# Two rows of v on SyncE's ring, a small transpose moved behind the K/Q transposes, the fp32 identity copied by VectorE, and four numbers of the scheduler's model altered

## Chip, cores and metric

One core of one Trainium2 chip. The metric is the device time of one execution in microseconds (us). Times are medians of several executions; a ratio is the mean time of one kernel's fast runs over the mean of the other's fast runs in the same rounds on the same chip, so it isn't quite the ratio of the medians quoted, and it carries a 95% interval. A difference counts as faster or slower from 2% on. A trace is of one single execution.

## The reference

Causal attention with a decay for 8 batches of 8 heads, 576 tokens and head size 64, then RMS norm and a gated feed-forward layer over the 4608 tokens.

```python
def _attn_ref(q, k, v, s):                       # q, k, v: (8, 8, 576, 64), s: (8, 8, 576)
    scores = scale * np.matmul(q, k.transpose(0, 1, 3, 2))
    cum = np.cumsum(np.maximum(s, 0.0), axis=-1)
    bias = -(cum[:, :, :, None] - cum[:, :, None, :])
    scores = np.where(causal, -1000000000.0, scores + np.minimum(bias, 0.0))
    ...                                          # softmax over keys
    return np.matmul(attn, v)

def _moe_ref(x, w_gate, w_val, w_out, rms_g):    # x: (4608, 512), d_ff 1536
    xn = x / np.sqrt(np.mean(x * x, axis=-1, keepdims=True) + 1e-06) * rms_g
    g = xn @ w_gate
    return (g * (1.0 / (1.0 + np.exp(-g))) * (xn @ w_val)) @ w_out
```

## The kernel before

The kernel isn't written in the order in which it runs. Every operation is recorded with the engine, a key (its priority) and modelled durations; a list scheduler plays the engines, the DMA and the PSUM banks through with these durations, and emits each engine's instructions in the order that it found. Where the model leaves TensorE idle in the first 24 us, `spin` puts fillers on a tile of zeros.

```python
class Plan:
    def schedule(self):                  # cut
        ...
            if o.dma:
                begin = max(self.dma_free, s + o.us + o.lags[0])
                self.dma_free = begin + o.dma
                o.done = self.dma_free + o.lags[1]

def load_runs(b, which, h0, h1, key, part=0):          # K (which 0) or Q (1) of four heads
    us = ((1.2, 1.25)[part] * (h1 - h0) / 4) if b == 0 else 3.05 * (h1 - h0) / 8
    return I("pool", "dma_start", 0.7, key=key, dma=us, lags=(1.1, 1.2), ...)

def prep_transpose(b, hp, key, part=0):                # K and Q of two heads, through PSUM
    mms(..., [...  ident_bf ...], key=key)             # then one copy by VectorE, one by ScalarE

# the beginning
kqa = [load_runs(0, w, h, h + 4, -100) for h in range(0, H, 4) for w in range(2)]
ident(ident_bf, -99.5)                                 # GpSimd
kqb = [load_runs(0, w, h, h + 4, -92, part=1) for h in (0, 4) for w in range(2)]
v0 = load_rows(v_nat[0], v, 0, "pool", -94)
ident(ident_F, -93.7)                                  # GpSimd
...                                                    # weight loads, fills by VectorE
wP = decay(-95)
for hp in range(HP):
    prep_transpose(0, hp, -80 + hp)
for hp in range(HP):
    prep_transpose(0, hp, -65 + hp, part=1)
gp_ = bank("g", 1)
mms(0.1, [(gp_[:, 0:CC], g4, ident_F[0:CC, 0:CC], True, True, True)], key=-75)
...
# per chunk c of 512 tokens: feed-forward, and beside it attention of batch c + 1
            if b < NRUN:                               # batch 1: K and Q transposed by TensorE
                for hp in range(HP):
                    prep_transpose(b, hp, K + hp)
            else:
                prep_cast(b, K - 14)                   # later batches: by DMA, on SyncE
...
                I("sp", "dma_start", 0.62, key=key, dma=0.75, out=out[rows, cols], in_=o[:, 0:w])

    def spin(b):
        nc.tensor.matmul(b[:, 0:256], lhsT=still[:, 0:128], rhs=still, start=True, stop=True)
```

## Time and profile before

| | before |
|---|---|
| time, median of 3 runs | 358.78 us (358.7 to 360.33) |
| span of the profiled run | 356.3 us |
| TensorE busy | 96% of the span |
| first K/Q transpose of batch 0 | 8.00 us |
| first feed-forward matmul | 23.50 us |
| K/Q transposes of batch 1 done | 44.49 us |
| feed-forward number 200, just behind the beginning of the second chunk | 68.82 us |
| last matmul ends | 351.95 us |

The feed-forward matmuls with the gate and value weights are counted in the trace (1248 of them) from 0 in order of start; the second chunk begins with number 192.

### The profile page before, as it was taken

What the parts mean: (1) busy time and instruction counts of PE and PEld (TensorE: products, weight loads), DVE (VectorE), ACT (ScalarE), POOL (GpSimd) and SP (SyncE); (2) the same over time, 40 slices, a digit from 0 to 9 for tenths busy, and PEclk for the clock granted to TensorE, in tenths of its full rate; (3) what the DMA queues carried; (4) which work ended last, traced back from release to release, by engine and by line L of the source; (5) the groups of instructions that cost most, each with busy time, mean ns of one, the idle gap of its engine ahead of it and who ended that gap; (6) DMA issues with size and microseconds to landing.
All of it is one profiled execution on the core that took longest, in us unless ns stands there. A gap on an engine that the chain in (4) does not pass through costs nothing.

```text
span 356.3 us, 8029 instructions
## 1 busy us (share of the span) xinstructions
PE 342.1 (96%) x3016; PEld 209.5 (59%) x3016; DVE 250.4 (70%) x495; ACT 229.8 (65%) x472; POOL 134.9 (38%) x217
## 2 busy tenths in 40 slices
PE   5988999999999999999999999999999999999995
PEld 4667775698569874887544454455445444444443
DVE  4678856698748995879687868887588657806840
ACT  2688899595777995857685668666898433224321
POOL 8996377321381349013910293029325100000000
PEclk9799999999999999999999999999999999999999
DMA  7999999999899997998999996889730250020002
GB/s 116 182 183 209 224 200 213 182 215 187 177 185 213 179 193 135 211 175 156 153 215 156 182 159 159 193 166 133 195 62 2 32 156 2 0 89 31 0 31 94
DMA packets 140613, 51.14 MB, mean 144 GB/s; under 512 B 127380, under 2 KB 135320, under 8 KB 140568
## 3 DMA queue, kind: packets, MB, share of 16 engines
q1 hardware_dynamic: 131832, 41.13, 60.7%
q0 software_dynamic: 8736, 9.44, 16.0%
q8 instruction: 25, 0.41, 0.5%
q14 instruction: 20, 0.16, 0.2%
HBM read 38.16 MB, written 9.44 MB: 134 GB/s over the span
## 4 chain that ended last, share of the span: by engine, by line
PE 84%; DVE 6%; POOL 3%; issue 3%; ACT 2%; DMA 1%; SPq 0%; POOLq 0%; ACTq 0%; DVEq 0%
PE psa L404 11%; PE psd L404 11%; PE pse L404 11%; PE psh L404 10%; PE psg L404 10%; PE psb L404 10%; PE psc L404 9%; PE psf L404 8%; DMA q_nat<-in_q_dram 1%; DVE x_blka L387 1%; DVE x_blkb L387 1%; POOL q_nat L387 1%; ACT Ee L387 1%; DVE Hs L387 1%; PE psd L843 1%
## 5 line engine op out<-in xcount | busy, mean ns | idle before, releaser
L404 PEld LDWEIGHTS <-wg_sb 128*128 128x128 bf16 x624 | 60.0, 98 | 33.8 <-issue 2.1
L404 PEld LDWEIGHTS <-wv_sb 128*128 128x128 bf16 x624 | 59.8, 98 | 32.3 <-issue 1.5
L404 PEld LDWEIGHTS <-Hs 128*128 128x128 bf16 x444 | 41.4, 98 | 42.5
L387 POOL TENSOR_SCALAR_AFFINE_SELECT Eb<-Eb 128x512 bf16<-128x512 bf16 x8 | 5.4, 679 | 80.7 <-ACT Eb L387 80.7
L387 POOL TENSOR_TENSOR vwb<-v_nata,wT 128x512 bf16<-128x512 f32 (+1 forms) x20 | 20.4, 1047 | 0.0
L387 ACT ACTIVATE sq_scr<-x_blkb 128x512 bf16<-128x512 bf16 x20 | 12.7, 633 | 11.7 <-DVE x_blkb L387 11.3
L387 DVE SCALAR_TENSOR_TENSOR x_blkb<-x_blkb,alb,gB 128x512 bf16<-128x512 bf16 x15 | 12.2, 862 | 10.7 <-POOL alb L387 10.7
L404 PE MATMUL psd<-wout_sb,Hs 128*128 128x512 bf16 (+1 forms) x84 | 18.5, 364 | 0.0
L404 PE MATMUL psa<-wout_sb,Hs 128*128 128x512 bf16 x72 | 17.8, 379 | 0.0
L404 PE MATMUL pse<-xnT,wg_sb 128*128 128x256 bf16 (+1 forms) x100 | 17.6, 311 | 0.2 <-DVE u_sba L387 0.2
L404 PE MATMUL psh<-xnT,wv_sb 128*128 128x256 bf16 (+1 forms) x100 | 17.5, 311 | 0.2 <-DVE x_blkb L387 0.2
L404 PE MATMUL psa<-xnT,wv_sb 128*128 128x256 bf16 (+1 forms) x104 | 17.6, 306 | 0.0
L387 ACT ACTIVATE sq_scr<-x_blka 128x512 bf16<-128x512 bf16 x18 | 11.3, 630 | 9.3 <-DVE x_blka L387 8.9
L404 PE MATMUL pse<-wout_sb,Hs 128*128 128x512 bf16 x72 | 17.2, 379 | 0.0
L404 PE MATMUL psf<-xnT,wg_sb 128*128 128x256 bf16 (+1 forms) x88 | 16.5, 321 | 0.6 <-DVE xnT L387 0.6
L404 PE MATMUL psb<-xnT,wv_sb 128*128 128x256 bf16 (+1 forms) x88 | 16.5, 321 | 0.0
L387 ACT ACTIVATE sq_scr<-q_bf 128x1024 bf16<-128x1024 bf16 (+1 forms) x18 | 16.4, 909 | 0.1
L387 ACT ACTIVATE sq_scr<-k_bf 128x1024 bf16<-128x1024 bf16 (+1 forms) x18 | 16.3, 908 | 0.0
L387 DVE CAST q_bf<-q_nat 128x512 bf16<-128x512 f32 (+1 forms) x30 | 16.0, 532 | 0.6 <-DMA q_nat<-in_q_dram 0.6
L387 POOL TENSOR_TENSOR vwa<-v_nata,wT 128x512 bf16<-128x512 f32 (+1 forms) x15 | 15.8, 1078 | 0.9 <-DMA v_nata<-in_v_dram 0.7
L404 PE MATMUL psd<-xnT,wv_sb 128*128 128x256 bf16 (+1 forms) x88 | 14.5, 302 | 0.0
L404 PE MATMUL psb<-xnT,wg_sb 128*128 128x256 bf16 (+1 forms) x88 | 14.5, 302 | 0.0
(471 smaller groups left out, 879.4 us busy)
## 6 DMA issues: line engine op xcount, KB each, us to landing
v_nata<-in_v_dram SPq DMA_DIRECT2D x24, 256.0 KB, 5.1
k_nat<-in_k_dram SPq DMA_DIRECT2D x24, 256.0 KB, 3.7
q_nat<-in_q_dram SPq DMA_DIRECT2D x24, 256.0 KB, 4.3
out_dram<-osba SPq DMA_DIRECT2D x12, 256.0 KB, 2.3
out_dram<-osbb SPq DMA_DIRECT2D x12, 256.0 KB, 2.5
out_dram<-osbc SPq DMA_DIRECT2D x11, 256.0 KB, 2.3
v_nata<-in_v_dram POOLq DMA_DIRECT2D x8, 256.0 KB, 10.4
wout_sb<-in_moe_w_out_dram POOLq DMA_DIRECT2D x2, 768.0 KB, 16.6
```

The source lines that it names most:

```text
L387: o = R.add(eng, us, lambda: f(**{n: real(a) for n, a in kw.items()}), outs, ins, key=key, lat=LAT[eng], kind=kind, dma=dma, name=outs[0]. ...
L404: nc.tensor.matmul(out, lhsT=lhsT, rhs=rhs, start=st, stop=sp)
L843: nc.tensor.matmul(b[:, 0:256], lhsT=still[:, 0:128], rhs=still, start=True, stop=True)
```

## The change

The intent: free the first K/Q transposes from a wait for the fp32 identity, which only the small rms_g transpose ahead of them needs; let GpSimd issue the second K/Q loads sooner by giving two of the v loads to SyncE; and have the identity from one VectorE copy. With it come fills that move behind the decay scan, and four altered numbers of the scheduler's model (K and Q loads 1.05 for 1.2 and 2.85 for 3.05, w_out 7.5 for 7.2, and lags for the other weights).

```diff
-        us = ((1.2, 1.25)[part] * (h1 - h0) / 4) if b == 0 else 3.05 * (h1 - h0) / 8
+        us = ((1.05, 1.25)[part] * (h1 - h0) / 4) if b == 0 else 2.85 * (h1 - h0) / 8
-            return I("pool", "dma_start", 0.84, key=key, dma=7.2 * (hi - lo) / 12,
+            return I("pool", "dma_start", 0.84, key=key, dma=7.5 * (hi - lo) / 12,
-        return I("pool", "dma_start", 0.76, key=key, dma=8.1 * (hi - lo) / DF,
+        return I("pool", "dma_start", 0.76, key=key, dma=8.1 * (hi - lo) / DF, lags=(1.2, 1.6),
...
-    v0 = load_rows(v_nat[0], v, 0, "pool", -94)
-    ident(ident_F, -93.7)
+    v0 = []
+    for c0, c1 in ((0, 1), (1, 2), (2, 3), (3, 4), (4, 5)):
+        n = 128 if c1 < 5 else 64
+        sp = c0 < 2
+        v0.append(I("sp" if sp else "pool", "dma_start", 0.5 if sp else 0.9, key=-94, ...))
+    I("dve", "tensor_copy", 0.15, key=-93.7, out=ident_F, in_=ident_bf)
...                                    (fills of KT, vw, mhalf, nrm: from ahead of the decay to behind its scan)
+    for o in fills:
+        R.after(o, R.ops[dec + 2])
+    kqt = [prep_transpose(0, hp, -80 + hp) for hp in range(HP)]
-    mms(0.1, [(gp_[:, 0:CC], g4, ident_F[0:CC, 0:CC], True, True, True)], key=-75)
+    o = mms(0.1, [(gp_[:, 0:CC], g4, ident_F[0:CC, 0:CC], True, True, True)], key=-75)
+    R.after(o, kqt[HP - 1])
```

More of the change, by code (lines that the diff above doesn't have):

```diff
@@ L462, in prep_transpose @@
         t = [lay(bank("kq", 4), bf16, "p (c t) -> p c t", n=KP * n, c=n) for w in range(2)]
-        mms(0.1 + 0.025 * n if b == 0 else 0.34,
+        mm = mms(0.1 + 0.025 * n if b == 0 else 0.34,
             [(t[w][64 * j : 64 * j + 64, c, :], raw[b][part][KP * w : KP * w + KP, 2 * hp + j, c, :],
@@ L473, in prep_transpose @@
                 I("act", "activation", 0.18 + 0.045 * n, key=key, out=o, in_=i, func=AF.Copy)
+        return mm
     def prep_cast(b, key):
@@ L770 @@
     kqb = [load_runs(0, w, h, h + 4, -92, part=1) for h in (0, 4) for w in range(2)]
-    v0 = load_rows(v_nat[0], v, 0, "pool", -94)
-    ident(ident_F, -93.7)
+    v0 = []
+    for c0, c1 in ((0, 1), (1, 2), (2, 3), (3, 4), (4, 5)):
+        n = 128 if c1 < 5 else 64
+        sp = c0 < 2
+        v0.append(I("sp" if sp else "pool", "dma_start", 0.5 if sp else 0.9, key=-94, dma=(c1 - c0) * 1.2 * n / 128,
+                    lags=(1.2, 1.2), out=v_nat[0][0:n, c0:c1],
+                    in_=v[0, :, c0 * 128 : c0 * 128 + (c1 - c0) * n, :].rearrange(
+                        "h (c p) d -> p c h d", p=n)))
+    I("dve", "tensor_copy", 0.15, key=-93.7, out=ident_F, in_=ident_bf)
     wl = []
@@ L776 @@
             wl.append(load_w(w, lo * 128, hi * 128, -93 + 0.1 * i))
+    dec = len(R.ops)
+    wP = decay(-95)
+    fills = []
     for t in KT:
-        fill("dve", t[:, :, S : NB * 128], 0.0, 0.17, key=-90)
+        fills.append(fill("dve", t[:, :, S : NB * 128], 0.0, 0.17, key=-90))
     for t in vw:
-        fill("dve", t[64:128, 4, :, :], 0.0, 0.5, key=-90)
-    fill("dve", mhalf, -0.5, 0.06, key=-90)
-    fill("dve", nrm, 0.0, 0.08, key=-90)
-    wP = decay(-95)
-    for hp in range(HP):
-        prep_transpose(0, hp, -80 + hp)
+        fills.append(fill("dve", t[64:128, 4, :, :], 0.0, 0.5, key=-90))
+    fills.append(fill("dve", mhalf, -0.5, 0.06, key=-90))
+    fills.append(fill("dve", nrm, 0.0, 0.08, key=-90))
+    for o in fills:
+        R.after(o, R.ops[dec + 2])
+    kqt = [prep_transpose(0, hp, -80 + hp) for hp in range(HP)]
     for hp in range(HP):
```

## The prediction

> **What bounds the kernel now.** I read the page first, then the kernel in stretches, the order of work in the first 32 us, the waits, and the time from issue to landing of each early load.
>
> Page, engines and slices (a slice is 8.9 us):
>
> ```profile
> PE 342.1 (96%) x3016; PEld 209.5 (59%) x3016; DVE 250.4 (70%) x495; ACT 229.8 (65%) x472; POOL 134.9 (38%) x217
> ...
> PE   5988999999999999999999999999999999999995
> ...
> PEclk9799999999999999999999999999999999999999
> ```
>
> TensorE is busy 96% of the span; no other engine passes 70%. So time can only be saved where TensorE does nothing useful. The stretches say where that is (busy us and count of each engine, granted clock, DMA share, GB/s):
>
> ```profile
> 0.00:32.10 32.10, 25.79 (x398) 19.01 (x399) 22.24 (x61) 19.19 (x43) 30.07 (x56) 0.89 1.04 168
> 32.10:62.00 29.90, 27.97 (x418) 21.24 (x416) 20.40 (x40) 27.78 (x56) 17.66 (x26) 1.00 1.15 212
> 62.00:100.00 38.00, 38.00 (x357) 28.19 (x356) 29.64 (x64) 27.11 (x56) 10.95 (x18) 1.00 1.04 189
> 100.00:180.00 80.00, 79.37 (x781) 58.48 (x780) 61.12 (x120) 60.33 (x127) 37.65 (x59) 1.00 1.02 177
> ```
>
> TensorE idles 6.3 us of the first 32.1, 1.9 of the next 29.9 and 0.6 of the 118 after that. The first stretch is worse than it looks: 62 of its 398 matmuls are fillers on a tile of zeros (line 843) that only keep the clock up. The first feed-forward matmul starts at 23.50. Before it there is load, transpose, scores, exp, mask, product with v and norm of the first batch, a chain of latencies; after about 32 us TensorE is the bound. The change works in the first 16 us, so its worth is the amount by which the 23.50, and the next starts, move forward.
>
> Order of work, 5 to 8 us (start, duration, engine, what, and the idle time before it):
>
> ```profile
> 4.77 0.49 PE L843 MATMUL psa<-still 128*128 128x256 bf16 x3
> 5.34 1.83 POOL L387 DMA_DIRECT2D v_nata<-in_v_dram  x2
> 7.15 0.23 POOL masks.py:197 MEMSET ident_F<- 128x128 f32 x1
> 7.46 0.29 POOL masks.py:199 TENSOR_SCALAR_AFFINE_SELECT ident_F<-ident_F 128x128 f32<-128x128 f32 x1
> 7.70 0.64 POOL L387 DMA_DIRECT2D q_nat<-in_k_dram  x1
> 7.80 0.26 PE L402 MATMUL psa<-ident_F,g 4*128 4x4 f32 x1 [2.54 <-POOL ident_F masks.py:199]
> ```
>
> GpSimd issues two v loads, then makes the fp32 identity, ready at 7.75. TensorE works in program order, and the small transpose of rms_g that needs this identity stands ahead of the K/Q transposes, which therefore start at 8.00. Their inputs were there earlier. Issue plus landing time gives K of heads 0-3 at 1.32 + 3.4 = 4.7, Q of them at 2.17 + 3.2 = 5.4, K and Q of heads 4-7 at 2.77 + 4.4 = 7.2 and 3.37 + 4.5 = 7.9; the bf16 identity ends at 5.37. So the first four heads stood ready for 2.6 us. There is a second cost:
>
> ```profile
> 6.00:8.00 2.00, 0.20 (x3) 0.18 (x3) 0.00 (x0) 0.28 (x1) 1.93 (x5) 0.83 0.99 159
> 8.00:10.00 2.00, 2.00 (x50) 1.63 (x53) 1.52 (x5) 0.94 (x3) 2.00 (x4) 0.50 0.87 206
> 10.00:12.00 2.00, 1.91 (x41) 1.00 (x41) 1.90 (x7) 2.00 (x7) 2.00 (x4) 0.50 1.18 138
> 12.00:14.00 2.00, 2.00 (x13) 0.98 (x12) 0.79 (x2) 1.85 (x6) 2.00 (x4) 0.50 1.22 196
> 14.00:16.00 2.00, 2.00 (x71) 1.81 (x70) 0.86 (x5) 0.20 (x1) 2.00 (x4) 0.96 1.08 244
> ```
>
> After the idle 2.5 us the granted clock is 0.5 from a little past 7 to a little past 14 us. And in the chain that ended last:
>
> ```profile
> 13.01 1.88 PE psd L843 x11
> ```
>
> Eleven fillers at half clock stand ahead of the first product with v (14.72).
>
> **What the Trainium skill says.** (1) "TensorE: Matmul & The Clock Gate", Part 1: the clock halves after an idle window of about 3.4 us and returns after a busy one; windows run free. The trace agrees in kind: half clock for about 6.8 us, two such windows, behind a window of which 5.26 to 7.3 was idle. (2) "DMA: Bandwidth & Descriptors", "Issuing engines are not separate DMA queues": loads from different engines share the same 16 DMA engines, and only issue time is saved. Here the DMA share at 4 to 8 us is already about 1, so I expect v on a second ring to slow K and Q. (3) Same page, "Queues, rings and completion order": each DMA engine takes turns between rings. No run yet shows two busy rings in this stage. (4) "SBUF — State Buffer", "Who interferes with whom": a VectorE copy in a two-port mode locks GpSimd out for its duration. For one copy of 128x128 that is a fraction of a microsecond.
>
> **The change part by part.**
> a) rms_g transpose behind the K/Q transposes. The 2.6 us wait of heads 0-3 goes. What replaces it is the landing of Q.
> b) v rows 0 and 1 from SyncE. Its first two issues end at 1.97 (1.46 + 0.51), nothing holds it afterwards, so the v loads go out at about 2.0 and 2.5, ahead of the second K/Q pair on GpSimd (2.77, 3.37). The first SyncE load, of s, landed 2.6 us after issue, so v packets should flow from about 3.4, just when K and Q do. Two v rows are as many bytes written (512 KB) as the four K/Q loads together, in 256-byte pieces. With even turns K0/Q0, partly through by then, lose about 0.9 us: Q0 lands at about 6.3 instead of 5.4 (estimate); K1/Q1 at about 9.2 instead of 7.9. v itself lands at about 7 to 9 instead of 5.34 + 4.4 = 9.7 and 11.4.
> So heads 0-3 start at about 6.4 instead of 8.0 (1.6 earlier), heads 4-7 at about 9.2 instead of 9.93 (0.7 earlier).
> c) GpSimd loses two issues (1.83) and the fp32 identity (0.23 + 0.29): the K/Q second-part issues start at 5.4 instead of 7.70, 2.3 us earlier. The bytes ahead of them are the same and the DMA engines are nearly full, so I count only 1 us on their landing (last one before: 9.54 + 6.8 = 16.3).
> d) The fp32 identity becomes one VectorE copy, about 0.2 us (the rms_g copy took 0.16, the 128x256 PSUM copies 0.42), at 5.4, where VectorE is idle. Decay transposes no longer wait for 7.75; the exp that feeds them ends at 6.27.
> e) The fills of KT, vw, mhalf, nrm (2 x 0.17, 2 x 0.49, 0.06, 0.10, some 1.5 us) go from 1.1-2.8 us, where VectorE was waiting for s, to behind the decay scan, 5.4 to about 7. They can stand ahead of the first KT copy: up to 0.4 us lost.
> f) Clock: the idle gap shrinks from 2.5 to about 1 us. If it stays at full clock, the fillers and about 100 small matmuls between 8 and 14 run faster; on the chain, part of the 1.88 us and a few tenths in transposes, perhaps 0.8 us.
>
> Sum for the first half (tokens 0-255): 1.6 - 0.4 + 0.5 (part of f) = about 1.7 us earlier. Second half: ScalarE is nearly full from 16 to 24 us (7.05 of 8) with its exps, whose inputs wait for the K/Q second part, so it gains the 1 us of (c). Where TensorE becomes the bound the gain is between them: about 1.5 us.
>
> **The rivals.**
> *The weights take over.* The first gate and value pieces landed at 15.02 + 5.2 = 20.2 and 15.79 + 6.1 = 21.9, against first use at 23.50 and 24.37; the second value piece at 27.0 against 28.44. With slack of only 1.4 to 2.5 us, and DMA bytes unchanged, a gain above about 2 us meets a DMA wait. For it: DMA share 1.0 to 1.2 up to 80 us. Against: GpSimd can issue the weights earlier too. It caps the time at about 356.5.
> *K/Q delayed by v so much that nothing is won.* If v's small pieces go first, Q0 lands after 7.2 and K1/Q1 after 10: heads 0-3 gain 0.8 and heads 4-7 nothing. Then 358.3. Against: the rings take turns.
> *The gain is kept in full and the clock stays up.* Then 2.6 plus 0.8 us or so, 355.4; it needs K and Q not slowed and weights earlier.
> *The new order of all later instructions* (each engine's order comes from a model whose load times were altered too) costs or gives some tenths up to 1 us by chance.
>
> **Range and chances.** 358.78 - 1.5 = 357.3; with a small weight for the full gain, 357.1. The rivals span 355.4 to 358.4, and the three runs before spread by 1.6 us, so 355.2 to 358.9. Two per cent are 7.2 us, more than the whole TensorE idle time of the first 32 us: faster by that 0.02, slower 0.01, within 0.97.
>
> **What would show it.** Right: first K/Q transposes at 6 to 7 us, no wait for the fp32 identity, clock 1.0 at 8 to 14, first feed-forward matmul at about 22, TensorE from 32 us on as before. Wrong: Q0 landing after 7.5; clock still halved; first feed-forward matmul past 23; or a start 2 us earlier with new TensorE waits for weights, K/Q or v of batch 1 (v landed at 46 to 51 us, its products with w followed at once) at 24 to 60 us that eat it.

## The result, and the profile after

The median is 363.34 us (362.51 to 364.09, 4 runs) against 358.74 us of before in the same rounds (358.62 to 360.33, 4 runs): ratio 1.0117, 95% interval 1.008 to 1.0154. Not 1.6 us faster, but 4.6 us slower. The spans are 361.3 and 356.3. Executions over 1.5% slower than the fastest of the same kernel are left out of the means. All outputs are right.

The page of the changed kernel, engines and slices (a slice is 9.0 us; the DMA share in later views is the packets' summed time over 16 engines, and can pass 1):

```profile
PE 343.9 (95%) x3002; PEld 208.7 (58%) x3002; DVE 252.1 (70%) x496; ACT 230.4 (64%) x472; POOL 128.4 (36%) x213
...
PE   7888898999999999999999999999999999999994
...
PEclk9699989999999999999999999999999999999999
```

TensorE has 1.8 us more busy time with 14 matmuls fewer, and its digits are lower at the second, fifth and seventh slice. The second lowered digit of the clock, at the sixth slice (45 to 54 us), wasn't there before. The same four stretches as in the prediction:

```profile
0.00:32.10 32.10, 26.15 (x382) 18.12 (x382) 23.60 (x63) 19.42 (x44) 24.93 (x47) 0.89 0.99 160
32.10:62.00 29.90, 26.32 (x389) 20.14 (x390) 16.94 (x32) 24.24 (x49) 15.93 (x28) 0.94 1.13 211
62.00:100.00 38.00, 37.56 (x351) 27.93 (x348) 31.75 (x68) 27.59 (x57) 10.99 (x18) 1.00 1.06 190
100.00:180.00 80.00, 78.59 (x777) 57.93 (x776) 61.22 (x116) 58.82 (x122) 37.64 (x59) 1.00 0.93 176
```

Against before, TensorE is busier by 0.36 us in the first stretch, and less busy by 1.65 us in the second, with the clock at 0.94 there instead of 1.00. This is the stage in which the prediction expected TensorE as before. The 100 to 180 stretch loses 0.8 us.

The first 16 us, TensorE and the waits (start, duration, engine, what, and in brackets the idle time before it and what ended it):

```profile
6.15 0.21 PE L402 MATMUL psa<-ident_bf,q_nat 64*64 64x64 bf16 x1
...
7.28 0.21 PE L402 MATMUL psb<-ident_bf,q_nat 64*64 64x64 bf16 x1 [0.92 <-DMA q_nat<-in_q_dram]
...
9.60 0.26 PE L402 MATMUL psh<-ident_bf,q_nat 64*64 64x64 bf16 x1 [0.61 <-DMA q_nat<-in_k_dram]
...
10.16 0.26 PE L402 MATMUL psb<-ident_bf,q_nat 64*64 64x64 bf16 x1 [0.30 <-DMA q_nat<-in_q_dram]
```

The wait for the identity is gone. In its place TensorE waits for K and Q: all transposes of the first heads but one begin at 7.28 (before: 8.00), the next at 9.60 and 10.16. From the issue times and the time from issue to landing, Q of heads 0-3 lands at 2.17 + 5.1 = 7.3 (before 5.4), K of heads 4-7 at 9.6 (7.2), Q at 10.2 (7.9). The v loads issued on SyncE from 2.01 on landed 4.7 us after issue. In the chain that ended last:

```profile
3.38 6.74 DMA q_nat<-in_q_dram
...
12.37 0.76 PE psc L855 x3
...
15.20 0.19 PE psf L402
```

The landing of Q (3.38 to 10.12) now stands in the chain, and right ahead of the products with v there are 3 fillers instead of 11. Two-us windows of the front:

```profile
6.00:8.00 2.00, 1.08 (x38) 0.57 (x35) 1.72 (x9) 1.10 (x3) 1.94 (x3) 1.00 1.46 195
8.00:10.00 2.00, 1.25 (x12) 0.69 (x11) 1.04 (x3) 0.68 (x3) 0.00 (x0) 0.82 1.39 193
10.00:12.00 2.00, 1.74 (x39) 1.15 (x41) 1.37 (x5) 1.34 (x5) 0.11 (x1) 0.50 1.35 238
12.00:14.00 2.00, 2.00 (x18) 1.04 (x14) 1.66 (x6) 1.76 (x7) 1.99 (x4) 0.50 0.31 74
14.00:16.00 2.00, 2.00 (x58) 1.57 (x58) 1.93 (x6) 1.11 (x3) 1.77 (x4) 0.50 0.49 131
```

The clock is halved here too, 9.29 to 16.11 instead of 7.32 to 14.15. The DMA share falls to 0.31 at 12 to 14 us because GpSimd sat in front of a mask that needs scores, with loads behind it in its order. GpSimd from 11.9 us on:

```profile
11.89 0.63 POOL L387 TENSOR_SCALAR_AFFINE_SELECT Ea<-Ea 128x512 bf16<-128x512 bf16 x1 [3.94 <-ACT Ea L387]
...
13.99 0.64 POOL L387 TENSOR_SCALAR_AFFINE_SELECT Ec<-Ec 128x512 bf16<-128x512 bf16 x1
14.86 0.63 POOL L387 TENSOR_SCALAR_AFFINE_SELECT Ed<-Ed 128x512 bf16<-128x512 bf16 x1 [0.23 <-ACT Ed L387]
```

And VectorE, first of the kernel before, then of the changed one:

```profile
10.38 0.16 DVE L387 TENSOR_TENSOR_SCAN ps<-ones,bs 64x3 f32<-64x3 f32 x1
10.57 0.15 DVE L387 SCALAR_TENSOR_TENSOR okr<-w_row,ps 64x3 f32<-64x3 f32 x1
...
15.11 0.18 DVE L387 RECIPROCAL rZa<-psd 128x4 f32<-128x4 f32 x1 [2.32 <-PE psd L404]
15.33 0.42 DVE L387 TENSOR_TENSOR x_blka<-psd,rZa 128x256 bf16<-128x256 f32 x1
```

```profile
13.49 0.18 DVE L387 RECIPROCAL rZa<-psc 128x4 f32<-128x4 f32 x1 [0.34 <-PE psc L404]
13.59 1.06 DVE L387 TENSOR_TENSOR_SCAN ps<-ones,bs 64x3 f32<-64x3 f32 x1
14.58 0.40 DVE L387 TENSOR_TENSOR x_blka<-psc,rZa 128x256 bf16<-128x256 f32 x1
14.91 0.59 DVE L387 SCALAR_TENSOR_TENSOR okr<-w_row,ps 64x3 f32<-64x3 f32 x1
```

The products with v begin 1.8 us earlier (12.91 for 14.72), yet their normalised result x_blka only 0.75 us earlier (14.58 for 15.33). In the new order two small operations of the decay (`ps`, `okr`) stand on either side of it. They took 0.16 and 0.15 us before; now `ps` runs from 13.59 to 14.65 and ends with the mask Ec of GpSimd (13.99 + 0.64 = 14.63), `okr` from 14.91 to 15.50 and ends with the mask Ed (14.86 + 0.63 = 15.49). That delay isn't what set the front, though: the chain above doesn't pass through `ps`. It runs through TensorE's products with v, with fillers between them, to the second K/Q transposes (`psf`). These stand in TensorE's order only at 15.13 (before: 15.37), although their data had landed between 10.7 and 13.0, and the first feed-forward matmul starts at 23.27: 0.23 us earlier than before, not 1.5.

Then the middle. TensorE at the transposes of batch 1, before and after, the one wait of its kind in each:

```profile
44.09 0.19 PE L402 MATMUL pse<-ident_bf,k_nat 64*64 64x64 bf16 x1 [0.65 <-issue]
```

```profile
45.52 0.21 PE L402 MATMUL psd<-ident_bf,k_nat 64*64 64x64 bf16 x1 [2.02 <-issue]
```

TensorE stands still for 0.65 us before and for 2.02 us after, within a row of identical transposes: 26 of the 144 were still to come before, 3 after. "issue" means that no semaphore wait shown by the profile ended it. Windows 44 to 47 and 47 to 50.5 of before, then of after (the number ahead of the DMA share is the clock):

```profile
44.00:47.00 3.00, 2.91 (x52) 2.25 (x52) 0.94 (x2) 2.41 (x6) 0.65 (x2) 1.00 1.05 221
47.00:50.50 3.50, 2.99 (x41) 2.21 (x40) 1.38 (x2) 3.50 (x8) 3.50 (x4) 1.00 1.22 172
```

```profile
44.00:47.00 3.00, 1.48 (x17) 1.09 (x19) 1.19 (x2) 1.06 (x2) 0.57 (x1) 0.97 1.13 262
47.00:50.50 3.50, 3.50 (x22) 2.23 (x18) 0.85 (x2) 2.55 (x5) 2.18 (x3) 0.54 1.15 191
```

After the pause the clock is halved from 46.83 to 50.25. Two groups of eight feed-forward matmuls there take 1.89 and 1.57 us instead of 1.04.

The whole loss by milestones, changed kernel less kernel before (start times in the two traces, end times in the rows that say so):

| stage ends with | before | after | lead (-) or lag | in this stage |
|---|---|---|---|---|
| first feed-forward matmul | 23.50 | 23.27 | -0.23 | -0.23 |
| batch-1 transposes begin | 39.91 | 39.72 | -0.19 | +0.04 |
| batch-1 transposes end | 44.49 | 45.74 | +1.25 | +1.44 |
| feed-forward number 200 (second chunk) | 68.82 | 72.04 | +3.22 | +1.97 |
| number 400 | 107.06 | 110.81 | +3.75 | +0.53 |
| number 600 | 145.72 | 150.09 | +4.37 | +0.62 |
| last matmul ends | 351.95 | 356.69 | +4.74 | +0.37 |
| span | 356.26 | 361.29 | +5.03 | +0.29 |

So there are three things to explain: a front that gained almost nothing, a stretch with a pause and a half clock in which the lag grows by 3.4 us, and 1.8 us trickling away later.

### The profile page after: what moved, and what is told of

The parts are those of the page before. It is cut to its first block, busy times and chain, and to the rows that moved or that the text cites. A ratio compares the mean times of both kernels' runs of the same rounds, so it can differ in the third digit from the quotient of the medians.

```text
span 361.3 us, 8001 instructions
## 1 busy us (share of the span) xinstructions
PE 343.9 (95%) x3002; PEld 208.7 (58%) x3002; DVE 252.1 (70%) x496; ACT 230.4 (64%) x472; POOL 128.4 (36%) x213
## 4 chain that ended last, share of the span: by engine, by line
PE 77%; DVE 8%; DMA 6%; POOL 3%; issue 2%; ACT 2%; SPq 0%; DVEq 0%; ACTq 0%; POOLq 0%
PE psh L404 12%; PE psa L404 10%; PE psd L404 10%; PE pse L404 9%; PE psc L404 9%; PE psf L404 9%; PE psg L404 8%; PE psb L404 8%; DMA wg_sb<-in_moe_w_gate_dram 3%; DMA q_nat<-in_q_dram 2%; DVE x_blka L387 2%; DVE Hs L387 1%; DVE u_sbb L387 1%; DVE x_blkb L387 1%; DMA k_nat<-in_k_dram 1%
## 5 line engine op out<-in xcount | busy, mean ns | idle before, releaser
L404 PE MATMUL psh<-wout_sb,Hs 128*128 128x512 bf16 x96 | 23.0, 379 | 0.0
L404 PE MATMUL psf<-xnT,wv_sb 128*128 128x256 bf16 (+1 forms) x100 | 18.4, 323 | 0.4 <-DMA wv_sb<-in_moe_w_val_dram 0.4
L387 DVE SCALAR_TENSOR_TENSOR x_blkb<-x_blkb,alb,gB 128x512 bf16<-128x512 bf16 x15 | 11.2, 795 | 10.6 <-POOL alb L387 10.6
L404 PE MATMUL psc<-xnT,wv_sb 128*128 128x256 bf16 (+1 forms) x108 | 17.6, 300 | 0.0
L404 PE MATMUL psh<-xnT,wg_sb 128*128 128x256 bf16 (+1 forms) x92 | 16.5, 314 | 0.0
L387 ACT ACTIVATE sq_scr<-q_bf 128x1024 bf16<-128x1024 bf16 (+1 forms) x18 | 16.4, 909 | 0.1
L387 ACT ACTIVATE sq_scr<-k_bf 128x1024 bf16<-128x1024 bf16 (+1 forms) x18 | 16.4, 910 | 0.0
L404 PE MATMUL psa<-xnT,wg_sb 128*128 128x256 bf16 (+1 forms) x92 | 15.5, 305 | 0.8 <-DMA wg_sb<-in_moe_w_gate_dram 0.8
L404 PE MATMUL psa<-xnT,wv_sb 128*128 128x256 bf16 (+1 forms) x80 | 15.5, 326 | 0.3 <-DVE u_sbb L387 0.3
L404 PE MATMUL pse<-xnT,wg_sb 128*128 128x256 bf16 (+1 forms) x84 | 15.5, 318 | 0.0
L404 PE MATMUL psc<-wout_sb,Hs 128*128 128x512 bf16 x60 | 15.1, 379 | 0.0
L404 PE MATMUL psg<-xnT,wg_sb 128*128 128x256 bf16 (+1 forms) x76 | 14.4, 323 | 0.6 <-DVE x_blkb L387 0.6
```

Of the source, the lines that this page charges most:

```text
L387: o = R.add(eng, us, lambda: f(**{n: real(a) for n, a in kw.items()}), outs, ins, key=key, lat=LAT[eng], kind=kind, dma=dma, name=outs[0]. ...
L404: nc.tensor.matmul(out, lhsT=lhsT, rhs=rhs, start=st, stop=sp)
```

## The experiments

Eighteen kernels ran. A few traces lack 12 or 13 records of feed-forward matmuls (undo_v, g_only, v_only, spins_short); for these no numbered milestone is used below, only the end of the batch-1 transposes and the end of the last matmul (the expectations call the same figure its start).

| kernel | median us (range, runs) | before beside it | ratio, 95% interval |
|---|---|---|---|
| undo_v | 359.44 (358.18-359.94, 6) | 358.35 | 1.0016 [0.9996, 1.0037] |
| g_only | 357.45 (356.95-358.30, 6) | 358.35 | 0.9966 [0.9947, 0.9985] |
| v_only | 357.70 (357.44-358.16, 6) | 358.35 | 0.9973 [0.9956, 0.9990] |
| spins_short | 361.50 (361.17-363.51, 6) | 358.35 | 1.0083 [1.0063, 1.0102] |
| feed | 365.10 (364.46-365.62, 5) | 358.42 | 1.0180 [1.0159, 1.0201] |
| spread | 360.01 (359.62-361.83, 6) | 358.42 | 1.0050 [1.0026, 1.0074] |
| const_only | 361.85 (360.72-362.65, 6) | 358.42 | 1.0094 [1.0071, 1.0117] |
| after_oldconst | 359.81 (357.86-361.00, 6) | 358.42 | 1.0026 [0.9999, 1.0053] |
| const_short | 361.87 (359.09-362.77, 6) | 359.22 | 1.0067 [1.0035, 1.0100] |
| g_short | 359.47 (356.63-360.36, 6) | 359.22 | 1.0000 [0.9967, 1.0032] |
| undo_short | 359.82 (357.03-361.13, 6) | 359.22 | 1.0021 [0.9985, 1.0056] |
| g_v | 359.25 (358.30-359.94, 6) | 359.22 | 1.0006 [0.9984, 1.0029] |
| before_out | 361.51 (360.94-363.68, 5) | 359.04 | 1.0065 [1.0043, 1.0087] |
| g_out | 359.79 (359.56-360.62, 4) | 359.04 | 1.0028 [1.0003, 1.0054] |
| g_short_out | 361.89 (359.54-365.05, 4) | 359.04 | 1.0112 [1.0052, 1.0172] |
| after_out | 362.31 (361.93-364.11, 4) | 359.04 | 1.0111 [1.0077, 1.0146] |
| g_short_mix | 360.01 (357.94-360.83, 6) | 358.49 | 1.0019 [0.9991, 1.0048] |
| g_mix | 359.01 (358.58-360.87, 6) | 358.49 | 1.0016 [0.9993, 1.0039] |

### The parts of the change, one at a time

**undo_v**: the change with the v rows issued by GpSimd again.

```diff
-        sp = c0 < 2
+        sp = False
```

> The changed kernel with the v rows of tokens 0-255 issued by GpSimd again, all else as changed. Theory 1 (v on the second ring takes the DMA engines from K and Q): Q of heads 0-3 lands at about 5.4 us as before instead of 7.27, second K/Q pair at 7.2 and 7.9 instead of 9.58 and 10.15, first K/Q transposes at about 5.7, and the first feed-forward matmul comes before 22.5 (23.27 in the changed kernel). Theory 2 (most of the loss is late: TensorE's 2.02 us stall at 43.5 us in the middle of the batch-1 transposes, and the half clock for 3.4 us behind it): the time follows that stall, whatever the front does: with a stall of 0.7 or less and no half clock about 358 to 360, with one of 2 us 362 to 363. Theory 3 (only the new order of instructions after 60 us costs): 362 to 363.5, no change.

Measured: 359.44 us. The first feed-forward matmul starts at 21.50, 1.8 us before the changed kernel and 2.0 before the old one. So without v on the second ring the front does what the prediction hoped for, and v on the second ring costs 1.8 us of it. The pause is still there (2.15 us, then a half clock from 43.85 to 47.27), and the last matmul ends at 353.92, later than before. The front isn't all that decides the end. Neither is the pause: theory 2 asked for 362 to 363 us with a pause of 2 us, and missed. By the ratios (1.0016 against 1.0117) this one edit gives back 3.6 us of the loss, with the four numbers still altered.

**g_only**: the kernel before, with the rms_g transpose behind the K/Q transposes and the identity by VectorE, and nothing else.

```diff
-    ident(ident_F, -93.7)
+    I("dve", "tensor_copy", 0.15, key=-93.7, out=ident_F, in_=ident_bf)
...
+    R.after(o, kqt[HP - 1])
```

> The kernel before with only two parts of the change: rms_g transpose behind the K/Q transposes, fp32 identity by VectorE. v stays on GpSimd, the fills and the model's load times stay. Theory 1: the wait of 2.5 us before the first transposes goes and nothing takes its place, so the first transposes start at 5.5 to 6 us, no half clock at 8 to 14 us, first feed-forward matmul 1 to 2 us before 23.50, time 356.5 to 358. Theory 2: 357 to 358.5 if the stall in the batch-1 transposes stays at about 0.65 us, up to 361 if it grows to 2. Theory 3 (any new order costs): 360 to 363.

Measured: 357.45 us, faster by 0.34% with an interval that excludes 1. First transpose 5.57, first feed-forward matmul 22.41 (before 23.50), clock not halved in the front; but the last matmul ends at 351.79, only 0.16 earlier. A gain of 1.1 us at 23 us has nearly gone at the end of the profiled run. The ratio over all runs still says 1.2 us, so the two single executions don't settle how much is lost.

**v_only**: the kernel before with the v loop of the change.

```diff
-    v0 = load_rows(v_nat[0], v, 0, "pool", -94)
+    v0 = []      # and the loop of the change
```

> The kernel before with only the two v rows moved to SyncE. The rms_g transpose still waits for the fp32 identity, which GpSimd now makes 1.8 us earlier (about 5.9). Theory 1: Q of heads 0-3 lands at about 7.3 us, K/Q transposes start at about 7.3, heads 4-7 at about 10.1, first feed-forward matmul at 23 to 24, DMA share below 0.6 for some us after 12, time 359 to 362. Theory 2: follows the stall at about 43 us, as in the other runs. If v on the ring were harmless: below 358.

Measured: 357.70 us, faster by 0.27%. Theory 1 expected 359 to 362 and missed, though Q of heads 0-3 landed at 7.4 as it said. The first transposes start at 7.15, and the first feed-forward matmul at 22.75, before the 23.50 of the kernel before.

**g_v**: both together, that is g_only with the v loop.

```diff
+    # g_only with
+    v0 = []      # and the loop of the change
```

> Both moves on the kernel before (v rows on SyncE; rms_g behind, fp32 identity by VectorE), with the fills and the load-time figures of before. Each alone was faster by 0.3%. If the two together are harmful by themselves (K and Q slowed, GpSimd waiting on a mask, DMA idle at 12-18 us): 359 to 362. If the loss of the change comes from the figures and fills and the order that they made: 356.5 to 358, with a stall below 1.2 us.

Measured: 359.25 us, ratio 1.0006. First feed-forward matmul 24.31, later than in either part alone and 1.9 us later than in g_only. The two parts don't add: the v loop costs 1.9 us of the front here, about as in the change (1.8 us, against undo_v), and gains 0.75 us on the kernel before. One thing differs in the traces: GpSimd issues the second K/Q loads at 4.66 instead of 6.24 in v_only, and K and Q of heads 4-7 land at 9.8 and 10.3 instead of 9.1 and 9.6. Whether that explains the 1.56 us between g_v and v_only wasn't tested.

**const_only**: the kernel before with nothing but the four numbers of the scheduler's model.

```diff
-        us = ((1.2, 1.25)[part] * (h1 - h0) / 4) if b == 0 else 3.05 * (h1 - h0) / 8
+        us = ((1.05, 1.25)[part] * (h1 - h0) / 4) if b == 0 else 2.85 * (h1 - h0) / 8
-                     dma=7.2 * (hi - lo) / 12,
+                     dma=7.5 * (hi - lo) / 12,
-                 dma=8.1 * (hi - lo) / DF,
+                 dma=8.1 * (hi - lo) / DF, lags=(1.2, 1.6),
```

> The kernel before with only the four load-time figures of the scheduling model changed (K/Q 1.05 and 2.85, w_out 7.5, weight lag 1.6). If a new order of the instructions alone costs time: 359.5 to 363. If the figures are harmless: 357.5 to 359.5, stall at the batch-1 transposes as before (0.6 to 0.9).

Measured: 361.85 us, slower by 0.94%. Four numbers that no instruction carries cost 3.4 us on the kernel before. The front even starts earlier (first feed-forward matmul 22.81), the pause is 2.27 us, no half clock follows it; lag against before +0.64 at the end of the batch-1 transposes, +0.98 at number 200, +2.12 at number 600, +3.10 at the last matmul. So two thirds of the lag come after 70 us; and const_short below, without the pause, costs as much within the intervals.

**after_oldconst**: the change with the four numbers as they were.

```diff
-        us = ((1.05, 1.25)[part] * (h1 - h0) / 4) if b == 0 else 2.85 * (h1 - h0) / 8
+        us = ((1.2, 1.25)[part] * (h1 - h0) / 4) if b == 0 else 3.05 * (h1 - h0) / 8
...                                    (and the other two lines)
```

> The changed kernel with the four load-time figures of before. If the figures and the order that they make are to blame: 357 to 359. If stall and half clock are (TensorE early, batch-1 K/Q late, so the fetch waits): the stall stays above 1.5 us and the time is 361 to 364.

Measured: 359.81 us, ratio 1.0026; 3.5 us of the 4.6 are given back (3.3 by the ratios). What is left agrees with g_v (1.0006) within the intervals; the two differ by the moved fills alone, so no cost of these is seen. The pause is still 2.11 us, without a half clock; 361 to 364 was expected with such a pause, and missed. The four numbers aren't needed for the pause.

The parts are no separate shares of the loss. By differences of the ratios, the numbers cost 0.94% on the kernel before, 0.91% in the change, and 0.50%, with the fills, on g_only (undo_v). The v loop gains 0.27% on the kernel before, costs 0.40% on g_only and 1.01% in the change. Undoing either one takes most of the loss away.

### What the pause is

**spins_short**: the change with each filler of 256 columns as two of 128. The work is the same, TensorE has two more instructions for each filler.

```diff
-        nc.tensor.matmul(b[:, 0:256], lhsT=still[:, 0:128], rhs=still, start=True, stop=True)
+        for _ in range(2):
+            nc.tensor.matmul(b[:, 0:128], lhsT=still[:, 0:128], rhs=still[:, 0:128], start=True, stop=True)
```

> The changed kernel with each filler matmul of 256 columns split into two of 128: same filler time, 96 more TensorE instructions before the batch-1 transposes, nothing else moved. Theory 2 in the form that TensorE waits for its instructions (the stall stands 256 instructions behind a fetch, at the same instruction number in both kernels, and ends 1.5 us after that fetch's transfer in both): the boundary now falls 96 instructions earlier, where the block before it holds 62 feed-forward instructions instead of 32 and so lasts about 1.3 us longer: stall at most 0.9 us instead of 2.02, no half clock at 47-50 us, time 359.5 to 361.5. If the stall comes from data, a buffer or a semaphore of the transposes, it stays at 2 us in the same place: 362.5 to 364.

The Trainium skill, "Runtime: NRT & Kernel Launch", section "Instruction fetch mechanics", says that each engine's instructions are streamed in blocks of 16 KiB, 256 instructions, and that the sequencer fetches the next block over a DMA queue of its own while it executes the current one. The traces agree: the page of the kernel before lists 25 transfers and 0.41 MB on an instruction queue, 16.4 KB each. The pause falls on the same instruction in every kernel with the long fillers, number 1217 of TensorE's list in the trace, though the fillers ahead of it number from 48 to 63; and the 256 instructions before it are mostly 64-column transposes, over in 3.3 us, while in the kernel before these transfers are mostly 7 to 20 us apart. The transfer that comes at that time, and the pause:

| kernel | block of 256 begins | transfer | TensorE stands | pause | resumes after the transfer's end by |
|---|---|---|---|---|---|
| before | 39.99 | 41.69-42.58 | 43.44-44.09 | 0.65 | 1.51 |
| after | 39.97 | 43.14-44.03 | 43.51-45.52 | 2.02 | 1.49 |
| undo_v | 38.06 | 41.38-42.27 | 41.60-43.76 | 2.15 | 1.48 |
| g_only | 38.88 | 40.55-41.45 | 42.34-43.13 | 0.79 | 1.68 |
| const_only | 39.11 | 42.47-43.36 | 42.57-44.84 | 2.27 | 1.48 |
| feed | 40.17 | 45.64-47.02 | 43.91-48.61 | 4.70 | 1.58 |

In 14 traces TensorE resumed 1.47 to 1.79 us after the end of that transfer, whatever the length of the pause. Measured in spins_short: the pause is gone, the batch-1 transposes end at 42.75 instead of 45.74, and no half clock follows. The transposes run without a break:

```profile
39.00:42.70 3.70, 3.70 (x166) 3.03 (x166) 3.28 (x6) 3.06 (x7) 0.99 (x2) 1.00 1.23 206
```

That shows that it was a wait for TensorE's own instructions: work, data and semaphores of that stage are the same, only the border of the block moved, to 50 transposes earlier. The block ahead of it now holds 31 feed-forward matmuls instead of 16 and lasts from 37.09 to 42.05, and the transfer (37.85-38.75) is over 3.3 us before it ends. The time followed only in part: 361.50 us, 1.8 below the change (1.2 by the ratios, whose intervals overlap), and not below before. The profiled run was the slowest of the six (363.51).

**feed**: the rival for the middle was that the weights and the loads of batch 1 come late because GpSimd idles (the 3.94 us above) in front of a mask. Here the masks of batch 0 stand behind the first loads.

```diff
-            masks[b, u] = I("pool", "affine_select", 0.59, key=-200 if b == 0 and u < HP else key, ...)
+            masks[b, u] = I("pool", "affine_select", 0.59, key=-92.95 if b == 0 and u < HP else key, ...)
```

> The changed kernel with the masks of the first half behind the last v rows and the first weight pair in GpSimd's order (mask key -92.95 instead of -200). Starving theory: in the changed kernel GpSimd sits 3.9 us at 8 to 12 us before a mask while loads wait behind it, the DMA share falls to 0.38 at 12-18 us, and all loads behind come later. Here the share at 12-18 us should be above 0.9, weights and batch-1 K/Q land 1 to 3 us earlier (last batch-1 K/Q at 39 to 41 instead of 42.0), no wait for weights at 28 and 32 us, and, as the fetch of TensorE's instructions started 0.7 to 1.1 us behind the landing of that last K/Q load in all six traces, the stall at the batch-1 transposes shrinks to 1.2 us or less: 359 to 361. If starving does not matter: 362.5 to 364 with the stall of 2 us.

Measured: 365.10 us, the slowest of all. The DMA share at 12 to 18 us rose from 0.38 to 1.30, and K and Q of batch 1 had landed by 37.9 instead of 42.0. So starved DMA wasn't the cause. The pause grew, and the clock was halved from 46.49 to 53.32:

```profile
48.61 0.26 PE L402 MATMUL psb<-ident_bf,k_nat 64*64 64x64 bf16 x1 [4.70 <-issue]
```

It ends 1.58 us after its transfer, as in the others; the transfer started only at 45.64. This also refutes what I had believed of the first six traces, that the transfer starts 0.7 to 1.1 us after the last K/Q load of batch 1 has landed: here it started 7.7 us after.

**spread**: the change with the transposes of batch 1 spread over more feed-forward work.

```diff
-                    prep_transpose(b, hp, K + hp)
+                    prep_transpose(b, hp, (K, K + 9, K + 11, K + 13)[hp])
```

> The changed kernel with the four head pairs' transposes of batch 1 given later keys, so that feed-forward matmuls stand between them: 180 instead of 216 transpose instructions in the 256 behind the fetch, some 1 to 1.5 us longer. Fetch theory: the stall at 43.5 us falls from 2.0 to 0.3 to 1.2 us and the half clock at 47-50 us is gone; time 359.5 to 362 (the transposes themselves come later, which may cost some of it). If the 3 us have another cause than stall and clock: 362.5 to 364.

Measured: 360.01 us, 3.3 below the change. The block that ends at instruction 1217 lasted 4.77 us instead of 3.3, and the pause fell to 1.08 with no half clock; the last matmul ends at 353.90. A longer block leaves less to wait for, as the reading of the pause says.

### Where the lead goes later

**const_short**, **g_short**, **undo_short**: const_only, g_only and undo_v with the fillers of spins_short (the same edit each time).

> The kernel before with the four changed load-time figures and with split fillers (the edit of spins_short). const_only took 361.85 with a stall of 2.27 us in the batch-1 transposes. If the fetch stall is what the figures cost: the 256 instructions behind the fetch now hold 94 feed-forward instructions instead of 32, the stall is 0 to 0.3, and the time falls by about 2 us to 359.5 to 360.3; the rest above 358.4 is the new order after 60 us. If the stall is harmless (other work would have waited anyway): 361 to 362.5.

> g_only (rms_g behind, fp32 identity by VectorE; 357.45) with split fillers. Its stall of 0.79 us should be 0: fetch theory 356.3 to 357.0. If the gain is eaten by a later wait, as the DMA order is unchanged: 357.2 to 357.8.

> undo_v (the change with v on GpSimd; 359.44) with split fillers. It had reached the batch-1 transposes 2.1 us before the kernel before and lost 4.6 us up to the second feed-forward stage, with a stall of 2.15 us and a half clock for 3.4 us behind it. Fetch theory: stall below 0.8, no half clock, so 3 to 3.5 us back: 356 to 357, faster than both kernels. If the loss is in the order of the instructions: 358.5 to 359.5.

All three lost the pause, and in none did the time fall clear of noise. const_short came out on its other branch (361 to 362.5), the pause being harmless there; g_short and undo_short lie above both of theirs:

| kernel | transposes of batch 1 end | number 200 | 400 | 600 | 400 to 600 | last matmul ends |
|---|---|---|---|---|---|---|
| before | 44.49 | 68.82 | 107.06 | 145.72 | 38.66 | 351.95 |
| const_only | 45.13 | 69.80 | 108.56 | 147.84 | 39.28 | 355.05 |
| const_short | 42.58 | 68.22 | 107.72 | 149.08 | 41.36 | 355.93 |
| g_short | 42.59 | 67.19 | 105.78 | 146.92 | 41.14 | 353.33 |
| undo_short | 41.12 | 67.65 | 106.56 | 145.02 | 38.46 | 352.82 |
| g_short_out | 42.71 | 67.03 | 105.80 | 145.28 | 39.48 | 351.24 |

Each row is one execution, and the six times of g_short alone spread from 356.63 to 360.36, so what follows holds for the execution traced. g_short is 1.3 us ahead of the kernel before at number 400 and 1.2 behind at number 600. The waits between 100 and 150 us say where (engine, what waited for what: us in total, times, longest), first of the kernel before, then of g_short:

```profile
ACT osbb L387 <- DMA out_dram<-osbb: 0.5, 1, 0.5
```

```profile
ACT osbb L387 <- DMA out_dram<-osbb: 3.8, 1, 3.8
...
PE psd L404 <- ACT osbb L387: 1.4, 1, 1.4
```

ScalarE can't evict the next output because the store of the buffer osbb isn't done, and TensorE can't go on because ScalarE's bank isn't free. SyncE's queue in g_short:

```profile
105.77 2.02 SPq L387 DMA_TRANSPOSE KTb<-k_bf  x1
107.89 1.21 SPq L387 DMA_TRANSPOSE QTb<-q_bf  x1
...
110.45 1.16 SPq L387 DMA_DIRECT2D out_dram<-osbb  x1
```

The filling of the buffer began at 94.3, 1.2 us earlier than in the kernel before (95.5), and its store was issued at 110.45, 1.4 us later (109.09): it stands behind the DMA transposes and loads of the next batches in SyncE's fixed order, and SyncE issues for about 55 of the 60 us from 60 to 120, in both. TensorE's lead didn't bring the store forward.

**g_short_out**: g_short with the output stores issued by GpSimd. The same edit makes **before_out**, **g_out** and **after_out** of the kernel before, of g_only and of the change.

```diff
-                I("sp", "dma_start", 0.62, key=key, dma=0.75, out=out[rows, cols], in_=o[:, 0:w])
+                I("pool", "dma_start", 0.9, key=key, dma=0.75, out=out[rows, cols], in_=o[:, 0:w])
```

> g_short (g_only with fillers of half the length in twice the number) with the output stores issued by GpSimd. This decides: g_short lost its lead of 1.3 us on the kernel before between feed-forward matmul 400 and 600 (41.1 us against 38.66), with TensorE waiting 1.38 us for ScalarE's osbb, which had waited 3.8 us for its store, issued late in SyncE's stream. Theory: without the stores in that stream, 400 to 600 takes under 39.3 us and the last matmul starts by 352.0 instead of 353.3. Rival (the lead is lost to the new order or to something else): 400 to 600 stays above 40.5.

> The kernel before, with the output stores issued by GpSimd instead of SyncE. Theory (SyncE's issue stream is a second limit: it issues for 55.5 of the 60 us from 60 to 120): SyncE has some 12 issues of about 0.45 us less in 60 to 120 us and idles visibly there; the kernel before itself waited only 0.5 us for a store, so the time moves by no more than 1 us either way (357.5 to 359.5) apart from the new order. Rival (the stream is paced by the transfers, not by the issues): SyncE stays full.

> g_only (rms_g transpose behind K/Q, identity by VectorE) with the output stores issued by GpSimd. Theory: the 1.9 us in which ScalarE waited for the store of osbb goes; start of the second half of the feed-forward work (number 400 to 600 of its matmuls) takes 38.6 us instead of 39.24, and the end lies some 0.5 us before that of g_only (351.8 last matmul, now 351.2). Rival (chance of the order): no such change, anywhere within 1.5 us.

> The change with the output stores issued by GpSimd. Its loss lies mainly before 72 us (stall and half clock in batch 1), which this does not touch, so theory: still 361 to 364, with 400 to 600 at 39.0 or less instead of 39.3. If the stall is set by what flows on the rings at 42 us, it stays as well: no store is out then. Rival (a good part of the loss is SyncE's stream): 359 to 360.

Measured in g_short_out: neither ScalarE nor TensorE waits for a store there any more, 400 to 600 takes 39.48 us instead of 41.14 (0.2 over what I had set, far from the rival's 40.5), and the last matmul ends at 351.24, 2.1 us before g_short and 0.7 before the kernel before. So in these traces the stores in SyncE's order took 1.66 of the 2.48 us that g_short lost there. The rest stays: in all six kernels with these stores on GpSimd 400 to 600 takes 39.48 to 39.54 us, also in before_out, where it was 38.66. As a kernel it is no gain: from the last matmul to the end it takes 6.54 us instead of 4.3 to 4.8, and its three fast runs spread from 359.5 to 363.2; the traced one is the fastest.

before_out missed: 361.51 us, outside the range I gave, with SyncE as full as before: 48 issues instead of 56, in about 56 of the 60 us; the DMA transposes took 27.5 us of it instead of 25.6. So here the rival held: fewer issues didn't empty SyncE. What made before_out slower wasn't isolated. g_out missed as well (400 to 600 39.48, expected 38.6). after_out stayed in its range, 362.31, with the pause of 2.02 us again, and 400 to 600 at 39.48, not the 39.0 expected: SyncE's stores have no part in the loss of the change that shows here.

**g_short_mix**, **g_mix**: g_short and g_only with the stores by GpSimd in all chunks but the last.

```diff
+                last = c == NCH - 1
-                I("sp", "dma_start", 0.62, ...)
+                I("sp" if last else "pool", "dma_start", 0.62 if last else 0.9, ...)
```

> g_short with the output stores issued by GpSimd in all chunks but the last, which SyncE stores again. In g_short_out the lead was kept (last matmul at 351.24 against 353.33 in g_short), but from the last matmul to the end it took 6.54 us instead of 4.3 to 4.8. Theory: that tail came from GpSimd's last store; here last matmul by 352.0, tail 4.3 to 4.8, span 356.0 to 356.8, time 357.5 to 358.5. Rival (the new order loses it elsewhere, as the spread of g_short_out's times, 359.5 to 365.1, may say): 359 to 361.

> g_only with the output stores issued by GpSimd in all chunks but the last. g_out had its last matmul at 351.64, 0.15 before g_only, and a tail of 6.54. Theory: last matmul at 351.6, tail 4.3, so 357.0 to 357.6, as g_only or 0.2 better. Rival: the new order costs something, 358.5 to 360.

Both missed: 360.01 and 359.01 us. The tail shrank only to 5.94 and 5.73 us, so GpSimd's last store was at most a part of it; and g_short_mix lost 1.69 us at 182 us, where TensorE waited for a DMA transpose of Q. Each removal of one wait showed the next one, and the spread of every one of these orders is larger than what is being looked for.

## Why the prediction was wrong, point by point

- **a) The wait for the identity goes.** Right. g_only alone shows it: transposes from 5.57, first feed-forward matmul 1.1 us earlier, 0.34% faster.
- **b) v slows K and Q.** Right in kind, too small in size, and the largest miss of the front: Q0 at 7.3, not 6.3; K1 and Q1 at 9.6 and 10.2, not 9.2. Those are nearly the numbers of its rival "K/Q delayed by v so much that nothing is won" (Q0 after 7.2, K1/Q1 after 10), and this is how the front went: 1.8 us at the first feed-forward matmul (change against undo_v), 1.9 (g_v against g_only).
- **c) The second K/Q parts.** They landed between 10.7 and 13.0 us, the last 3.4 us earlier than before instead of 1, and weren't used before 15.13, as TensorE's order held them back.
- **d) and e)** Right in size, though the fills came 0.9 us later than said. The last fill ended at 7.93 and the first KT copy started at 7.85, 0.2 us after the first ScalarE copy of the same transposes.
- **f) The clock.** Wrong for the change: halved for as long as before, 2 us later. Right for g_only, where it stayed up.
- **The sum.** 0.23 us earlier at the first feed-forward matmul, not 1.5 to 1.7. The mis-sized term is b): with v back on GpSimd (undo_v) the front is 2.0 us earlier. Two of the prediction's signs of being wrong came true here: the clock still halved, and the first feed-forward matmul past 23. (Two slips in the working changed nothing: the first gate piece had 3.3 us of slack, 20.2 to 23.50, not 1.4 to 2.5; and the rivals as given end at 358.3, not 358.4.)
- **"TensorE from 32 us on as before".** This is one step that failed. A front that gains nothing would have given 358.5. The pause at the batch-1 transposes was in the trace of before (0.65 us, ended by "issue"), and I had not looked at it; with the half clock behind it, it stands in the stretch that lost 3.4 us, between 39.7 and 72 us. How much of that it costs at the end isn't settled: without the pause (spins_short) the ratio falls by 0.34%, within the intervals, and undo_v and after_oldconst keep a pause of over 2 us at 1.0016 and 1.0026. A wait for instructions isn't in any list of semaphores or buffers, and so in none of my rivals.
- **"The new order of all later instructions costs or gives some tenths up to 1 us by chance".** This is the other step that failed: I saw the four numbers and gave them at most 1 us. const_only shows 3.4 us (+0.94%) for them alone, after_oldconst gives 3.3 us of the change's loss back by the ratios. They aren't the whole cause: taking v off SyncE's ring (undo_v) gives back 3.6 us with the numbers left in. "By chance" holds as far as is known: nothing in the diff says in which direction.
- **The gain is capped later.** The prediction named the weights as the cap. New waits for weights did come (0.43 and 0.77 us at 28.4 and 31.9), but what was seen to eat a lead is the store in SyncE's order at 107 to 120 us, in g_short and not in the change itself (g_short, g_short_out, after_out).

What stays open. Why the transfer of instructions starts 0.8 to 5.5 us after the block before it has begun: the lag is 1.5 to 1.7 us in the kernel before, g_only and g_out and about 3.3 in the change, undo_v and const_only, and neither the landing of K and Q nor the DMA share orders it (1.12 to 1.26 in the first 2 us of the block, in all 14 traces). Nor is it shown when the half clock follows a pause: after 2.02 to 2.27 us of pause it came in two kernels (the change, undo_v) and not in three (const_only, after_oldconst, after_out). And for the 2.1 us that const_only loses after 70 us no single wait was isolated.

## What to carry to other kernels

Where a scheduler emits the order, a changed number in its model is a change to the kernel: run it alone, with all else as it was, before crediting or blaming the edit beside it. Two edits that gain alone can cancel each other (0.34% and 0.27%, together a ratio of 1.0006); so run each alone and both. And when an engine pauses at the same instruction number with no semaphore to name, ask how fast it runs through its instructions there, before asking for data.

## What the Trainium skill lacked or had wrong

- "Runtime: NRT & Kernel Launch", "Instruction fetch mechanics", calls the cost of a block border mostly hidden. Behind a block that TensorE went through in 3.3 to 4.8 us it was 0.44 to 4.70 us, and TensorE resumed 1.47 to 1.79 us after the transfer's end in 14 traces; no figure for that latency is given, nor for how long after the block's beginning the transfer starts (1.5 to 5.5 us in these traces).
- "DMA: Bandwidth & Descriptors", "Issuing engines are not separate DMA queues", says that a second issuing engine only saves time on the sequencer. Here it moved two v rows ahead and delayed others' loads: the first K and Q of batch 0 landed 0.9 to 2.4 us later. By how much the other ring's loads are delayed isn't given there.
- "SBUF — State Buffer", "Who interferes with whom", speaks of a lock for an operation's duration. The runs show its size for tiny operations: a VectorE scan of 64x3 elements took 1.06 us instead of 0.16 and ended with GpSimd's mask (14.65 and 14.63). In seven traces twelve of the operations `ps` and its `okr` took 0.27 to 1.07 us, each ending within 0.03 us of a mask's end; all others took 0.14 to 0.19. The other way round, GpSimd's select for the bf16 identity took 1.03 us in the kernel before and ended 0.09 us after VectorE's scan of 64x576, and 0.29 us in the change, where that scan came later: a gain of some 0.7 us for the second K/Q loads that the prediction didn't have.
